# Gate products by groups of 32 tokens, turned by VectorE, in a windowed attention with a routed mixture of experts

## The chip, the cores and the metric

The kernel runs on one core of a Trainium2 chip. A core has five engines with their own instruction streams: TensorE (matmuls, PE in the profile, with its weight loads as PEld), VectorE (DVE), ScalarE (ACT), GpSimd (POOL) and SyncE (SP, which here only issues DMAs). SBUF is the working memory with 128 partitions, PSUM the memory into which TensorE writes. The metric is the time of one execution in microseconds (us); lower is better.

## What is computed

Sliding-window causal attention over 8 batches, 8 heads, 576 tokens and 64 dimensions a head, and on its output x (4608 tokens of 512 values) a mixture of eight experts with one expert for each token. Which one it is follows from two products of x with small weights: eight logits, and a local gate that says whether the token keeps the expert of the token before it.

```python
rel = pos[:, None] - pos[None, :]
mask = (rel >= 0) & (rel < window)            # window = 64
attn = softmax(where(mask, scale * q @ k.T, -1e9))
x = (attn @ v), heads side by side            # (B, S, 512)
logits = x @ w_gate                           # 8 of them
local_gate = sigmoid(x @ w_local)
for b, s:
    fresh_e = argmax(logits[b, s])
    e = fresh_e if s == 0 or local_gate[b, s] < 0.5 else prev_e
    prev_e = e
    out[b, s] = softmax(logits[b, s])[e] * (relu(x[b, s] @ w1[e]) @ w2[e])
```

## The kernel before

**Stages.** Attention comes first, over nine chunks of 512 tokens (`sc` from 0 to 8), each in four units of two heads (`hp` from 0 to 3). The router then makes places for the tokens, and the experts run over blocks of 256 gathered tokens, the first of them while the router still works on the rest. The order of the instructions on TensorE, ScalarE and SyncE is the order in which attention's code issues them; the instructions of VectorE and GpSimd are ordered by the scheduler of the framework.

**A unit.** `scores` makes k.T q for two heads in blocks of 64 by 64 (line 385), ScalarE takes the exponential (line 416) and VectorE multiplies by the mask (line 421; for seven units the mask is added by matmuls instead, line 400). `values` multiplies with v (line 431, 32 matmul records of a unit in pairs), and VectorE divides by the sums (lines 436, 439 and 441). Scores run two units ahead of values. `shift` copies v to a second tile that starts 64 tokens earlier, on ScalarE and GpSimd (lines 360 to 367).

**The gates, two ways.** Nine numbers are wanted for each token: eight logits and the local gate. For chunks 0 to 3, x itself is turned by TensorE (`turn`, line 302, copied by ScalarE at line 305), and `gates` multiplies it with the weights in four matmuls of 512 columns, one for each pair of heads (line 315). For chunks 4 to 8 (`GATED`), v is loaded already turned (`vtt`), and `gates` multiplies it with the weights of each head (line 317): 16 numbers a head, nine of them used, which then ride along with v through attention as nine more columns of `va` and `vb`. In both cases the four matmuls write to 32 PSUM partitions each, so that partitions hold gates and columns hold tokens. ScalarE copies this to `gs` (line 318).

**Turning them back.** The readers want tokens in partitions. `back` does four 128x128 transposes on TensorE (line 332). For chunks 0 to 3, `logits` sums the four pairs of heads on VectorE into `lt` (line 338); for chunks 4 to 8, `spread` has ScalarE copy the numbers into the free columns of `vb` and `va` (lines 346 to 348). The 64 tokens ahead of chunk 4 are treated alone by `gates_ahead` (lines 325 and 327) and `back_ahead` (lines 352 and 353), and a GpSimd copy puts them in place (line 345). All of these and the router's small products share one PSUM bank (`bank`).

**Places in the order.** For a chunk below 4, `gates` is issued at the end of the unit `hp` = 1 of the next chunk and `logits` in unit 2. For a gated chunk, `gates` is issued at the end of unit 2 of the chunk ahead of it and `spread` in unit 3, behind that unit's next scores. The router's first part (`first` and `gate`, lines 774 to 1025) is issued in small steps between units from chunk 4 on; its products at lines 812, 822 and 845 are TensorE instructions in the same stream, and its table at line 980 as well. It reads `lt`.

**Loads.** SyncE issues the loads of q, k, v and the turned v, up to three chunks ahead, and from about 112 us the first expert's weights (line 1182).

Of the kernel before, what the change touches and what calls it, by code (L numbers as in the profile page):

```python
# [8 lines left out]
F32 = mybir.dt.float32  # L9
# [4 lines left out]
Alu = mybir.AluOpType  # L14
AX = mybir.AxisListType
# [4 lines left out]
P = 128  # L20
B, H, S, DH = 8, 8, 576, 64
D = H * DH
E, F = 8, 1024
DK, FK = D // P, F // P
WIN = 64
# [35 lines left out]
SC = 4 * P  # L61
NSC = N // SC
HP = H // 2
KB = SC // WIN
SB = S // WIN
GW = 32
VX = DH + 1
VW = VX + E + 1
GATED = range(4, NSC)
# [8 lines left out]
def row_of(t):  # L78

    return t + (t >= ZR)  # L80
# [87 lines left out]
def attention(ctx, tc, ring, kq, v3, v4, vt, vh, xs, lt, ok, wg, wg2, ident, rt, ex):  # L168
# [14 lines left out]
    nc = tc.nc  # L183
    tp = ctx.enter_context(tc.tile_pool(name="at_t", bufs=1))
    cp = ctx.enter_context(tc.tile_pool(name="at_const", bufs=1))
    kp = ctx.enter_context(tc.tile_pool(name="at_k", bufs=3))
    pp = ctx.enter_context(tc.tile_pool(name="at_p", bufs=LEAD + 3))
    wk = ctx.enter_context(tc.tile_pool(name="at_work", bufs=2))
# [11 lines left out]
    def bank():  # L200

        return ps_e.tile([P, SC], F32, name="r")
# [3 lines left out]
    kqs, qts, kts, vts, vas, vbs = {}, {}, {}, {}, {}, {}  # L206
# [6 lines left out]


    vhs = tp.tile([P, HP, SC], F32, name="vtt")[:, :, :WIN]
    ahead = cp.tile([P, WIN], F32, name="ahead")
    ahead_t = cp.tile([P, H, E + 1], F32, name="ahead_t")

    def load(sc, parts):
        for part in parts:  # L220
# [16 lines left out]
    def until(i, x):  # L237

        nc.sync.dma_start(out=late[:, i:i + 1], in_=x)
# [57 lines left out]
    def turn(sc, x, half):  # L297

        r = pair()
        for i in range(2):  # L300
            for c in range(4):
                nc.tensor.transpose(r[:, i, c * P:(c + 1) * P],
                                    x[:, c, 2 * half + i].rearrange("p j d -> p (j d)"), ident)
        o = pp.tile([P, 2, SC], F32, name="p")
        nc.scalar.copy(o, r)
        vts.setdefault(sc, []).append(o)

    def gates(sc):

        r = bank()  # L310
        gs = wk.tile([P, SC], F32, name="gs", bufs=1)
        for hp in range(HP):
            h = slice(hp * GW, (hp + 1) * GW)
            if sc not in GATED:
                nc.tensor.matmul(r[h, :], lhsT=wg[:, hp, :], rhs=vts[sc][hp // 2][:, hp % 2], start=True, stop=True)
                continue
            nc.tensor.matmul(r[h, :], lhsT=wg2[:, hp, :], rhs=vts[sc][:, hp, :], start=True, stop=True)
        nc.scalar.copy(gs, r)
        return gs

    def gates_ahead():

        r = bank()
        for hp in range(HP):
            nc.tensor.matmul(r[hp * GW:(hp + 1) * GW, :WIN], lhsT=wg2[:, hp, :], rhs=vhs[:, hp, :],
                             start=True, stop=True)
        nc.scalar.copy(ahead, r[:, :WIN])

    def back(gs):
        r = bank()  # L330
        for c in range(4):
            nc.tensor.transpose(r[:, c * P:(c + 1) * P], gs[:, c * P:(c + 1) * P], ident)
        return r

    def logits(sc, gated):

        gt = back(gated).rearrange("p (c h g) -> p c g h", c=4, h=HP)[:, :, :E + 1]
        nc.vector.tensor_reduce(lt[:, 4 * sc:4 * sc + 4, :], gt, axis=AX.X, op=Alu.add)

    def spread(sc, gated):  # L340

        gt = back(gated).rearrange("p (c h g) -> p c h g", c=4, h=H)[:, :, :, :E + 1]
        g = slice(VX, VW)
        if sc == GATED[0]:
            nc.gpsimd.tensor_copy(vbs[sc][WIN:, 0, :, g], ahead_t[WIN:])
        nc.scalar.copy(vbs[sc][:WIN, :, :, g], gt[:WIN])
        nc.scalar.copy(vbs[sc][WIN:, 1:, :, g], gt[WIN:, :3])
        nc.scalar.copy(vas[sc][:, :, :, g], gt)

    def back_ahead():  # L350
        o = bank()[:WIN, :P]
        nc.tensor.transpose(o, ahead, ident)
        nc.scalar.copy(ahead_t[WIN:], o.rearrange("p (h g) -> p h g", h=H)[:, :, :E + 1])

    def shift(sc):

        va = vas[sc]
        vb = vbs[sc] = space("vb", sc)
        w = slice(width(sc - 1))
        nc.scalar.copy(vb[WIN:, 0, :, w], vas[sc - 1][WIN:, 3])  # L360
        nc.gpsimd.tensor_copy(vb[:WIN, :2], va[:WIN, :2])
        yield
        nc.scalar.copy(vb[WIN:, 1:3], va[WIN:, :2])
        yield
        nc.gpsimd.tensor_copy(vb[:WIN, 2:], va[:WIN, 2:])
        yield
        nc.scalar.copy(vb[WIN:, 3], va[WIN:, 2])

    def shift_first(half):

        va, h = vas[0], slice(4 * half, 4 * half + 4)
        if not half:
            vbs[0] = space("vb", 0)
            nc.gpsimd.memset(vbs[0][WIN:, 0], 0.0)
        nc.gpsimd.tensor_copy(vbs[0][:WIN, :, h], va[:WIN, :, h])
        nc.scalar.copy(vbs[0][WIN:, 1:, h], va[WIN:, :3, h])
# [78 lines left out]
    moves, gated, turned, old = (), None, None, None  # L455
# [3 lines left out]
    def step(free=True):  # L459
        nonlocal pause, side, trip  # L460
        pause -= HALF

        if side and pause <= 0.0 and (free or not trip):
            w, trip = next(side, (0.0, None))
            pause = max(pause, -HALF) + w
            if trip is None:
                side = ()
                if ex.jobs:
                    ex.rows(ex.jobs[0], -1)

    for i, (sc, hp) in enumerate(units):
        if hp == 0:
            x, g = wk.tile([P, 4, HP, 2, DH], F32, name="x"), None
            if sc in GATED:
                g = wk.tile([P, 4, HP, 2, E + 1], F32, name="g")

        if 1 < i < len(units) - LEAD:
            ps[units[i + LEAD]] = scores(*units[i + LEAD])
        if hp == (0 if sc else 3) and sc + 1 < NSC:
            moves = shift(sc + 1)  # L480
        for _ in range(2 if sc else 4):
            next(moves, None) if moves else None

        if hp == 3 and sc + 1 in GATED:
            spread(sc + 1, gated)
        elif (sc, hp) == (1, 3):
            gates_ahead()
        elif (sc, hp) == (2, 3):
            back_ahead()
        if hp == 3 and sc not in GATED:  # L490
            turn(sc, x, 0)
            old = x
        elif sc and sc - 1 not in GATED:
            if hp == 0:
                turn(sc - 1, old, 1)
            elif hp == 2:
                logits(sc - 1, turned)

        if side is None and 4 * sc >= C1 and hp >= 2:
            side = rt.first(bank)  # L500
        step(not (hp == 3 and sc + 1 in GATED))
        values(sc, hp, ps.pop((sc, hp)), x, g)
        if i < 2:
            ps[units[i + LEAD]] = scores(*units[i + LEAD])
        if i == 0:
            shift_first(1)
            until(1, allr[:1, 0, 0, 0, :1])
            load(2, [pairs[0], whole, pairs[1]])
            nc.sync.dma_start(out=vhs, in_=vh)
            load(3, pairs)  # L510
        if i == 2 * HP:
            with tc.issue_after(masked[-1].ins):
                rt.prepare()
                build_bias()
        if hp == 1 and sc and sc - 1 not in GATED:
            turned = gates(sc - 1)
        if hp == 2 and sc + 1 in GATED:
            gated = gates(sc + 1)
        if 0 < sc < NSC - 2 and hp == 0:
            load(sc + 2, [whole])  # L520
        if 0 < sc < NSC - 3 and hp == 1:
            load(sc + 3, pairs)
        if hp == 2 and sc + 2 in GATED:
            load(sc + 2, ["turned"])
        if (sc, hp) == (NSC - 3, 3):
            ex.jobs = [ex.weights({}, -1, ("w1",), lambda: until(2, allr[:1, sc, hp, 0, :1]))]
            if side == ():
                ex.rows(ex.jobs[0], -1)
        step(not (hp == 2 and sc + 1 in GATED))
        if (sc, hp) == (NSC - 2, 1):  # L530
            ex.weights(ex.jobs[0], -1, ("w2",), lambda: until(3, allr[:1, sc, hp, 0, :1]))
        if hp == HP - 1:
            if sc in GATED:
                nc.vector.tensor_reduce(lt[:, 4 * sc:4 * sc + 4, :], g.rearrange("p c h j e -> p c e (h j)"),
                                        axis=AX.X, op=Alu.add)
            nc.gpsimd.dma_start(out=xs[row_of(sc * SC):row_of(sc * SC) + SC, :D].rearrange("(c p) d -> p c d", p=P),
                                in_=x.rearrange("p c h j d -> p c (h j d)"))
# [1081 lines left out]
```

## Time and profile before

| | us |
|---|---|
| median of three runs | 644.74 |
| lowest and highest | 644.02, 646.02 |
| the profiled execution | 642.1 |
| its span, first to last instruction | 640.0 |
| TensorE busy | 615.6 |
| VectorE busy | 402.3 |
| ScalarE busy | 200.6 |
| attention's last values (line 431) end at | 133.5 |

The profile is of one execution. Times in it run from the start of the span. A row of the timeline gives the start, the duration, the engine, the line, the operation, the tiles it writes and reads, and in brackets how long the engine was idle before it and what ended that. "issue" in this place means that no semaphore, and so no other work of the program, ended the wait. A matmul's end is modelled, so for the time that TensorE spends on a group the start of the next group is the better guide. Engines overlap; what counts is the chain that cannot start earlier. A float32 matmul shows as two weight loads and two matmuls, a float32 transpose as one of each.

### The profile page before, as it was taken

The numbers are of one execution on the slowest core, as the hardware profiler recorded it, in microseconds if no ns is written. First come the engines' busy times: TensorE is split into PE (matmuls) and PEld (weight loads), VectorE is DVE, ScalarE is ACT, GpSimd is POOL, SyncE is SP. The second block draws the span as 40 slices with busy tenths as digits, with TensorE's granted clock in tenths as the row PEclk, the third lists the DMA queues.
The fourth block names the chain that finished last, engine by engine and source line by source line (L and its number), as shares of the span: only waits on it lengthen the run. The fifth ranks groups of instructions, "written<-read, shape, count | busy, mean of one in ns | idle before, by whom it ended". The sixth has DMA issues, their size and how long they took to land. (4 is left out here: it accounts for less than half of the span.)

```text
span 640.0 us, 14994 instructions
## 1 busy us (share of the span) xinstructions
PE 615.6 (96%) x6367; PEld 544.2 (85%) x6367; DVE 402.3 (63%) x752; ACT 200.6 (31%) x368; POOL 133.1 (21%) x132
## 2 busy tenths in 40 slices
PE   8889998899999999999999999999999999999995
PEld 7777777788889999978997999887997998899994
DVE  6676588879968775273654683362917752886730
ACT  3766765612572122113120312021211221213120
POOL 5422112430103202120302120211312022111101
PEclk9999998999999999999999999999999999999998
DMA  9999996969757645786958665769768556956501
GB/s 338 416 418 406 385 366 241 348 236 337 237 171 246 244 166 198 242 316 236 387 189 291 218 234 212 259 235 367 263 228 324 185 199 232 379 167 225 209 17 38
DMA packets 29318, 166.43 MB, mean 260 GB/s; under 512 B 8451, under 2 KB 9497, under 8 KB 20026
## 3 DMA queue, kind: packets, MB, share of 16 engines
q1 hardware_dynamic: 20394, 135.54, 58.4%
q0 software_dynamic: 8848, 29.85, 12.2%
q8 instruction: 52, 0.85, 0.5%
q14 instruction: 24, 0.20, 0.1%
HBM read 146.18 MB, written 19.59 MB: 259 GB/s over the span
## 5 line engine op out<-in xcount | busy, mean ns | idle before, releaser
L1394 POOL DMA_INDIRECT out_dram<-y,idx x36 | 41.1, 1141 | 339.1 <-DVE y L1327 196.5
L1318 PE MATMUL hp<-ws,hs 128*128 128x256 f32 x384 | 88.7, 380 | 0.0
L1318 PEld LDWEIGHTS hp<-ws,hs 128*128 128x128 f32 x384 | 72.6, 190 | 10.5 <-issue 0.8
L1268 PE MATMUL hp<-xs,ws 128*128 128x128 f32 x672 | 79.6, 275 | 0.0
L1268 PEld LDWEIGHTS hp<-xs,ws 128*128 128x128 f32 x672 | 77.3, 192 | 0.0
L1327 DVE SCALAR_TENSOR_TENSOR y<-hp,xg,kept 128x256 f32<-128x256 f32 x48 | 22.6, 482 | 74.2 <-issue 47.0
L1414 PE MATMUL hp<-xt,w 128*64 128x64 f32 (+2 forms) x640 | 66.2, 276 | 0.0
L1414 PEld LDWEIGHTS hp<-xt,w 128*128 128x128 f32 (+1 forms) x640 | 60.8, 170 | 4.1 <-issue 0.7
L1318 PE MATMUL hp<-w,h 128*128 128x256 f32 x256 | 61.1, 382 | 0.0
L1162 POOL DMA_INDIRECT xg<-xs,gx x40 | 50.3, 1258 | 45.6 <-issue 37.4
L1279 DVE TENSOR_TENSOR h<-hp,keep 128x512 f32<-128x512 f32 x42 | 28.6, 690 | 48.1 <-PE hp L1268 48.0
L1268 PEld LDWEIGHTS hp<-xt,w 128*128 128x128 f32 x448 | 53.2, 192 | 2.7 <-issue 1.3
L1268 PE MATMUL hp<-xt,w 128*128 128x128 f32 x448 | 54.7, 275 | 0.0
L1318 PEld LDWEIGHTS hp<-w,h 128*128 128x128 f32 x256 | 47.2, 190 | 6.3 <-issue 0.4
L431 PE MATMUL xo<-vb,p 128*64 128x74 f32 (+1 forms) x576 | 44.5, 230 | 7.0 <-issue 2.9
L416 ACT ACTIVATE p<-sp 128x512 f32<-128x512 f32 x72 | 39.2, 595 | 38.0 <-PE sp L385 35.9
L385 PEld LDWEIGHTS sp<-w 64*64 64x64 f32 x1296 | 38.7, 138 | 12.1 <-issue 8.5
L421 DVE TENSOR_TENSOR p<-p,mask 128x1024 f32<-128x1024 f32 x29 | 36.1, 1245 | 19.5 <-ACT p L416 19.3
L431 PEld LDWEIGHTS xo<-vb,p 128*64 128x64 f32 x576 | 38.9, 138 | 9.9 <-issue 4.4
L385 PE MATMUL sp<-w 64*64 64x128 f32 (+1 forms) x1296 | 43.8, 270 | 2.6 <-issue 1.5
L431 PE MATMUL xo<-va,p 128*64 128x74 f32 (+1 forms) x576 | 44.5, 230 | 1.2 <-issue 1.2
L1280 ACT ACTIVATE h<-h 128x512 f32<-128x512 f32 x42 | 26.3, 630 | 59.1 <-DVE h L1279 59.1
(280 smaller groups left out, 955.0 us busy)
## 6 DMA issues: line engine op xcount, KB each, us to landing
w<-in_w_dram SPq DMA_DIRECT2D x42, 2048.0 KB, 9.2
w<-in_kq_dram SPq DMA_DIRECT2D x17, 1024.0 KB, 8.7
w<-in_w_dram SPq DMA_DIRECT2D x24, 512.0 KB, 9.3
xs<-x POOLq DMA_DIRECT2D x9, 1024.0 KB, 9.5
va<-in_v_dram SPq DMA_DIRECT2D x5, 1184.0 KB, 8.9
vtt<-in_vt_dram SPq DMA_DIRECT2D x5, 1024.0 KB, 7.2
va<-in_v_dram SPq DMA_DIRECT2D x3, 1040.0 KB, 12.2
va<-in_v_dram SPq DMA_DIRECT2D x2, 520.0 KB, 6.8
```

The costliest lines, as they stand in the source:

```text
L385: nc.tensor.matmul(sp[j][c * WIN:(c + 1) * WIN, a:b], lhsT=kt[h, hp, block * WIN:(block + 1) * WIN], rhs=qt[h, hp, a:b], start=not biased, ...
L416: nc.scalar.activation(p[:, j], sp[j], Act.Exp, scale=DH ** -0.5)
L421: masked.append(nc.vector.tensor_tensor(p, p, m.to_broadcast([P, 2, SC]), op=Alu.mult))
L431: nc.tensor.matmul(xo[par * WIN:(par + 1) * WIN, j, s * VW:s * VW + n], lhsT=p[:, j, b * WIN:(b + 1) * WIN], rhs=w[:, s, 2 * hp + j, :n], ...
L1162: asked = self.nc.gpsimd.indirect_dma_start(out=x, out_offset=None, in_=self.xs[:rows, :], in_offset=bass.IndirectOffsetOnAxis(ap=gx[:, s: ...
L1268: nc.tensor.matmul(out[:, m, :], lhsT=a[:, kk, m * P:(m + 1) * P], rhs=b[:, kk, :], start=start and m + kk == 0, stop=stop and (m, kk) == ...
L1279: nc.vector.tensor_tensor(o, x, y, op=add)
L1280: nc.scalar.activation(o, x if y is None else o, Act.Relu)
L1318: nc.tensor.matmul(out, lhsT=a[:, m, :], rhs=b[:, m, :], start=start and m == 0, stop=stop and m == FK // 2 - 1, skip_group_check=True)
L1327: nc.vector.scalar_tensor_tensor(y[i][:, j * w:(j + 1) * w], x, pw[i], y2, Alu.mult, Alu.add)
L1394: self.nc.gpsimd.indirect_dma_start(out=self.out[:, :], out_offset=bass.IndirectOffsetOnAxis(ap=st["idx"][:, s:s + 1], axis=0), in_=y, in_ ...
L1414: nc.tensor.matmul(hp[a, i, :], lhsT=st["w1"][:, kk, m * P:(m + 1) * P][:, a], rhs=st["xt"][:, kk, :n], start=(kk == 0), stop=(kk == DK - 1))
```

## The change

The gate products are made so that VectorE's transpose of blocks of 32 by 32 suffices to turn them. The 512 tokens of a chunk are taken as 4 x 4 x 32 (c, q, t): a matmul takes the tokens of one q, 128 of them, and writes the 32 gates of a pair of heads to the PSUM partitions of that q. That makes sixteen matmuls of 128 columns in place of four of 512. For chunks 0 to 3 the four pairs of heads add up in PSUM, in 128 columns. One VectorE transpose reads PSUM and writes `gs` with tokens in partitions. `back`, `back_ahead` and ScalarE's copies of the gates go. `logits` becomes one ScalarE copy from `gs`, `spread` copies from `gs` in place of PSUM, and `gates_ahead` makes eight matmuls of 32 columns and a VectorE transpose of 64 partitions.

```diff
-    ahead = cp.tile([P, WIN], F32, name="ahead")
-    ahead_t = cp.tile([P, H, E + 1], F32, name="ahead_t")
+    ahead = cp.tile([P, P], F32, name="ahead")
...
     def gates(sc):
-        r = bank()
-        gs = wk.tile([P, SC], F32, name="gs", bufs=1)
+        r, gs = bank(), wk.tile([P, SC], F32, name="gs", bufs=1)
         for hp in range(HP):
-            h = slice(hp * GW, (hp + 1) * GW)
-            if sc not in GATED:
-                nc.tensor.matmul(r[h, :], lhsT=wg[:, hp, :], rhs=vts[sc][hp // 2][:, hp % 2], start=True, stop=True)
-                continue
-            nc.tensor.matmul(r[h, :], lhsT=wg2[:, hp, :], rhs=vts[sc][:, hp, :], start=True, stop=True)
-        nc.scalar.copy(gs, r)
+            x = vts[sc][:, hp] if sc in GATED else vts[sc][hp // 2][:, hp % 2]
+            x = x.rearrange("p (c q t) -> p q c t", c=4, q=4)
+            for q in range(4):
+                a = slice(q * GW, (q + 1) * GW)
+                if sc in GATED:
+                    nc.tensor.matmul(r[a, hp * P:(hp + 1) * P], lhsT=wg2[:, hp, :], rhs=x[:, q], start=True, stop=True)
+                else:
+                    nc.tensor.matmul(r[a, :P], lhsT=wg[:, hp, :], rhs=x[:, q], start=hp == 0, stop=hp == HP - 1,
+                                     skip_group_check=True)
+        if sc in GATED:
+            nc.vector.transpose(gs.rearrange("p (c h g) -> p h c g", c=4, h=HP),
+                                r.rearrange("p (h c t) -> p h c t", c=4, h=HP))
+        else:
+            nc.vector.transpose(gs[:, :P], r[:, :P])
         return gs

     def gates_ahead():
         r = bank()
         for hp in range(HP):
-            nc.tensor.matmul(r[hp * GW:(hp + 1) * GW, :WIN], lhsT=wg2[:, hp, :], rhs=vhs[:, hp, :],
-                             start=True, stop=True)
-        nc.scalar.copy(ahead, r[:, :WIN])
-    def back(gs):
-        r = bank()
-        for c in range(4):
-            nc.tensor.transpose(r[:, c * P:(c + 1) * P], gs[:, c * P:(c + 1) * P], ident)
-        return r
+            for i in range(2):
+                a = slice(WIN + i * GW, WIN + (i + 1) * GW)
+                nc.tensor.matmul(r[a, hp * GW:(hp + 1) * GW], lhsT=wg2[:, hp, :], rhs=vhs[:, hp, i * GW:(i + 1) * GW],
+                                 start=True, stop=True)
+        nc.vector.transpose(ahead[WIN:], r[WIN:, :P])

     def logits(sc, gated):
-        gt = back(gated).rearrange("p (c h g) -> p c g h", c=4, h=HP)[:, :, :E + 1]
-        nc.vector.tensor_reduce(lt[:, 4 * sc:4 * sc + 4, :], gt, axis=AX.X, op=Alu.add)
+        nc.scalar.copy(lt[:, 4 * sc:4 * sc + 4, :], gated[:, :P].rearrange("p (c g) -> p c g", c=4)[:, :, :E + 1])

     def spread(sc, gated):
-        gt = back(gated).rearrange("p (c h g) -> p c h g", c=4, h=H)[:, :, :, :E + 1]
+        gt = gated.rearrange("p (c h g) -> p c h g", c=4, h=H)[:, :, :, :E + 1]
         g = slice(VX, VW)
         if sc == GATED[0]:
-            nc.gpsimd.tensor_copy(vbs[sc][WIN:, 0, :, g], ahead_t[WIN:])
+            nc.gpsimd.tensor_copy(vbs[sc][WIN:, 0, :, g],
+                                  ahead[WIN:].rearrange("p (h g) -> p h g", h=H)[:, :, :E + 1])
...
-    def back_ahead():
-        o = bank()[:WIN, :P]
-        nc.tensor.transpose(o, ahead, ident)
-        nc.scalar.copy(ahead_t[WIN:], o.rearrange("p (h g) -> p h g", h=H)[:, :, :E + 1])
...
-        elif (sc, hp) == (2, 3):
-            back_ahead()
```

## The prediction

> **What bounds the kernel now.** I read the page first, then TensorE's idle times, then stretches cut where TensorE stood still. The page says that TensorE is busy nearly all the time and that a queue of its own brings instructions: 52 packets of 0.85 MB in all, 16 KB each.
>
> ```profile
> PE 615.6 (96%) x6367; PEld 544.2 (85%) x6367; DVE 402.3 (63%) x752; ACT 200.6 (31%) x368; POOL 133.1 (21%) x132
> ...
> q8 instruction: 52, 0.85, 0.5%
> ```
>
> The change lies wholly in attention, the first 131 us. The waits of TensorE (matmuls; engine, line, who ended it: us, times, longest) are few, and the largest one is of kind "issue": TensorE waited for nothing that the profile shows.
>
> ```profile
> PE xo L431 <- issue: 4.1, 4, 1.8
> ...
> PE xo L431 <- DVE x L441: 2.5, 1, 2.5
> ...
> PE sp L385 <- issue: 1.5, 2, 1.1
> ...
> PE r L822 <- DVE loc L817: 0.9, 1, 0.9
> PE r L812 <- ACT va L348: 0.6, 1, 0.6
> PE hp L1268 <- DVE h L1279: 0.5, 2, 0.2
> ```
>
> Where do the "issue" waits stand? In the timeline they cut groups in the middle: nothing that a data dependence would choose.
>
> ```profile
> 33.91 0.27 PE L431 MATMUL xo<-vb,p 128*64 128x65 f32 x1 [0.65 <-issue]
> ...
> 39.90 0.27 PE L385 MATMUL sp<-w 64*64 64x64 f32 x2 [1.09 <-issue]
> ...
> 122.94 0.22 PE L431 MATMUL xo<-va,p 128*64 128x74 f32 x1 [1.19 <-issue]
> ```
>
> I asked for the stretches from one such restart to the next (us; then PE and PEld with their instructions; the last two columns are the DMA share and GB/s).
>
> ```profile
> 27.71:33.91 6.20, 5.55 (x128) 4.20 (x128) 3.23 (x5) 3.78 (x7) 1.70 (x2) 1.00 1.01 423
> 33.91:39.90 5.99, 4.90 (x127) 4.30 (x128) 3.31 (x6) 2.80 (x5) 1.91 (x2) 1.00 1.02 423
> 39.90:52.24 12.34, 11.66 (x255) 9.48 (x255) 10.64 (x34) 8.73 (x14) 1.74 (x4) 1.00 1.01 415
> 122.94:129.11 6.17, 4.42 (x127) 4.03 (x127) 4.71 (x9) 2.17 (x4) 0.81 (x1) 1.00 1.02 409
> ...
> 52.24:121.60 69.36, 63.91 (x1528) 51.80 (x1528) 51.59 (x146) 45.22 (x80) 19.39 (x18) 0.98 0.93 339
> ```
>
> Each stretch holds 254 to 256 of TensorE's instructions, matmuls and weight loads together (the third holds two such blocks), and a packet of that queue, 0.85 MB / 52, would be 256 instructions of 64 bytes. Between 31.2 and 32.5 us, just ahead of the restart at 33.91, one passes:
>
> ```profile
> q8 instruction: 1, 0.02, 5.1%
> ```
>
> So I read the stalls as TensorE waiting for its next 256 instructions while the DMA engines are full. From 27.71 to 52.24 us a block costs 24.53/4 = 6.13 us however quickly TensorE works it off, 24 ns an instruction. From 52.24 to 121.60 us 3056 instructions, with some semaphore waits twelve blocks, take 69.36/12 = 5.78 us each, with no such stall: here TensorE's work, VectorE's chain and the fetch run at nearly one pace. After 115 us the experts' weights are loaded and the fetch binds again.
>
> **What the change does to TensorE.** One gate stage and what follows it, in the timeline of all engines and then in that of TensorE:
>
> ```profile
> 62.62 0.16 PEld L317 LDWEIGHTS r<-vtt,wg2s 128*32 128x32 f32 x8
> 62.62 1.07 PE L317 MATMUL r<-vtt,wg2s 128*32 128x512 f32 x8
> ...
> 63.62 0.99 PEld L385 LDWEIGHTS sp<-w 64*64 64x64 f32 x36 [0.84 <-issue]
> 63.62 1.13 PE L385 MATMUL sp<-w 64*64 64x128 f32 x36
> ...
> 64.67 0.42 PEld L332 LDWEIGHTS r<-ident,gs 128*128 128x128 f32 x4
> 64.67 0.66 PE L332 MATMUL r<-ident,gs 128*128 128x128 f32 x4
> ...
> 65.92 1.23 DVE L421 TENSOR_TENSOR p<-p,mask 128x1024 f32<-128x1024 f32 x1 [1.64 <-ACT p L416]
> ...
> 31.76 0.66 PE L332 MATMUL r<-ident,gs 128*128 128x128 f32 x4
> ...
> 32.14 0.27 PE L332 MATMUL r<-ident,gs 128*128 128x128 f32 x1
> 32.34 0.27 PE L431 MATMUL xo<-vb,p 128*64 128x65 f32 x1
> ```
>
> Removed: four transposes, in whose place nothing could start for 32.34 - 31.76 = 0.58 us. In nine stages that is 5.2 us of TensorE's time.
>
> Replaced: four matmuls of 512 columns by sixteen of 128. The old ones took 63.62 - 62.62 = 1.00 us. The new ones stream as many columns over the same four column groups, but are 64 instructions where the old were 16 (each float32 matmul shows two loads and two matmuls). The scores behind them issue 72 instructions in 64.67 - 63.62 = 1.05 us, 14.6 ns each; 64 of them make 0.93 us. The other end is eight rounds of the 0.27 us of a lone 128-column matmul, 2.2 us, if rounds do not overlap; the scores, which overlap, are the nearer row. I take 1.00 us, no change.
>
> So a stage goes from 16 + 8 to 64 instructions, 40 more; nine stages make 360. The first chunk's earlier gates go from 16 + 2 to 32, 14 more. Together 374, or 1.46 blocks.
>
> **The other engines.** No row shows VectorE's transpose. Near it are copies and products of the same sizes:
>
> ```profile
> L1197 DVE COPY xt<-tp 128x512 f32<-128x512 f32 x5 | 3.2, 682 | 0.0
> ...
> L439 DVE TENSOR_TENSOR g<-xo,allr 128x72 f32<-128x72 f32 x20 | 4.6, 232 | 0.5
> ...
> L318 ACT COPY gs<-r 128x512 f32<-128x512 f32 x9 | 5.3, 585 | 7.4 <-PE r L317 5.8 <-PE r L315 1.6
> ...
> L338 DVE TENSOR_REDUCE lt<-r 128x36 f32<-128x144 f32 x4 | 1.2, 306 | 2.9 <-PE r L332 2.9
> ...
> L327 ACT COPY ahead<-r 128x64 f32<-128x64 f32 x1 | 0.2, 220 | 0.0
> ```
>
> I take 0.68 us for 128x512, five times (bounds 0.59, ScalarE's copy of the same tile, and 1.23, the mask product of twice the size; the copy from PSUM by the same engine is the nearest row), and 0.3 us for 128x128, four times, against the 0.31 us of the reduction that goes. ScalarE loses nine copies of 0.585 us and gains four of about 0.22 us; it is 31% busy, so I count nothing. The new waits: VectorE's transpose waits for the gates, and behind it the next mask stands; in the stage above VectorE idles 1.64 us ahead of that mask, which covers 0.68. ScalarE's copies of the gates now wait for VectorE where they waited for TensorE; behind them stand copies and exponentials of a later unit. The PSUM bank is free sooner, so L812's 0.6 us goes, but the router's numbers that L812 and L822 carry come from VectorE, which is late instead.
>
> Two places hand savings to VectorE:
>
> ```profile
> 81.53 0.21 DVE L436 RECIPROCAL allr<-xo 128x8 f32<-128x8 f32 x1 [1.09 <-PE xo L431]
> ...
> 84.38 0.17 PE L822 MATMUL r<-ident,loc 14*1 14x14 f32 x1 [0.93 <-DVE loc L817]
> ...
> 102.18 0.28 PE L431 MATMUL xo<-vb,p 128*64 128x74 f32 x1 [2.52 <-DVE x L441]
> ...
> 100.00:105.00 5.00, 2.82 (x54) 2.67 (x58) 4.97 (x17) 1.87 (x4) 0.75 (x1) 0.76 0.55 219
> ```
>
> At 84.38 VectorE had idled 1.09 us shortly before; 0.68 of transpose plus TensorE coming 0.58 us sooner use that up, so the stage ahead of it saves nothing. At 102.18 TensorE already waits 2.52 us for VectorE: that stage's 0.58 us is lost, and its transpose lengthens the wait by 0.68. Given back: 0.58 + 0.58 + 0.68 = 1.84 us. The granted clock is 0.76 there after the wait; I count nothing for a longer one.
>
> **The sum by stretches.** To 52.24 us, two stages and the early gates: 94 instructions at 24 ns, +2.25 us; TensorE's saving is not felt, since the fetch sets the pace. From 52 to 115 us, six stages: -6 x 0.58 + 1.84 = -1.64 us; but 240 more instructions in 1.64 us less leave 67.7/12.9 = 5.25 us for a block. A block's fetch costs at most 5.78 us there on average, so the loss is between 0 and 12.9 x 0.53 = 6.8 us; I take a sixth, 1.1 us, because no stall shows there today. The DMA load is lower too:
>
> ```profile
> DMA packets 2729, 14.57 MB, mean 416 GB/s; under 512 B 742, under 2 KB 742, under 8 KB 1254
> ...
> DMA packets 2501, 15.97 MB, mean 380 GB/s; under 512 B 234, under 2 KB 234, under 8 KB 1002
> ```
>
> (20 to 55 us and 55 to 97 us.) That makes -0.5 us. After 115 us, one stage: 40 x 24 ns = +0.95 us. Sum: 2.25 - 0.5 + 0.95 = **+2.7 us**. Behind attention the list of waits has nothing over the 0.5 us of L1268, so a delay passes through to the end. The profiled execution took 642.1 us (span 640.0), 2.6 below the median of 644.74; I carry the difference to the median: **647.4 us**.
>
> **Rivals.** *The fetch stays hidden.* Then TensorE's work decides: -9 x 0.58 + 1.84 = -3.4 us, 641.3. It wins if a block costs under 5.25 us; for it speaks that twelve blocks run without a stall, against it the stalls at 6.0 to 6.2 us. [...]
>
> *The fetch gives way.* A slower pace asks less of the DMA engines, and an early block falls from 6.13 to 5.78 us: 4.37 x 5.78 - 24.53 = +0.7, the middle -0.5, the end between -0.58 and +0.95, say +0.2: +0.4 us, 645.1. Against it: the early transfers are asked for well ahead and keep the queues full.
>
> *The fetch binds throughout.* All 12.9 blocks at 5.78 us: 2.25 + 6.8 - 1.64 + 0.95 = +8.4 us, 653.1.
>
> That the sixteen matmuls do not run four abreast is the 2.2 us end above: nine times 1.2 us, +10.8 us. I leave it inside the tail.
>
> **How the numbers follow.** Forecast 0.38 (its own range 645.3 to 649.5), hidden 0.24, gives way 0.26, binds throughout 0.12. A measurement of this kernel tells 0.3%, 1.9 us, from no change. Of the forecast I put 0.06 within that; of the second rival 0.02 below it. Faster 0.26, same 0.30, slower 0.44. The range 641.3 to 651.5 leaves out half of the first rival and two thirds of the third.
>
> **What would show it.** Right: in the profile after, restarts "<-issue" inside groups, more of them than now and now also between 52 and 115 us, 256 instructions apart, in sum well over the 5.6 us of the two rows above; q8 with one or two packets more; the sixteen matmuls in about 1.0 us. VectorE's transpose near 0.68 us and the wait at L431 near 102 us longer. Wrong: no "issue" waits between 52 and 115 us and an attention that ends before 129 us; gates of over 1.2 us; or a transpose above 1 us, which would make VectorE the bound.

## The result and the profile after

The changed kernel takes **651.86 us** (median of six runs, 649.62 to 654.65) against 644.79 us (median of six, 643.69 to 646.76) for the kernel before: a ratio of 1.0109, with a 95% interval of 1.0079 to 1.0139, or 7 us slower. The forecast was 647.4 us with a range to 651.5: the sign was right, the loss was two and a half times as large. The profiled execution of after is the slowest of its six (654.65 us, span 652.7), 2.8 us above their median, and that of before (642.1 us, span 640.0) lies 2.7 us below its own. So the two traces differ by 12.6 us where the medians differ by 7.1, and a difference read between them is too large by some us.

What was added is there to the instruction. The page of after, busy times and TensorE's instruction queue (packets, MB):

```profile
PE 616.0 (94%) x6554; PEld 550.0 (84%) x6554; DVE 405.5 (62%) x758; ACT 196.9 (30%) x361; POOL 131.5 (20%) x132
...
q8 instruction: 54, 0.88, 0.5%
```

187 matmuls and 187 loads more, 374 together, and two packets more. One gated stage in the timeline of after shows the sixteen matmuls from 66.12 to 67.13 us, 1.01 us like the four, and no transposes on TensorE behind the scores:

```profile
66.12 0.81 PEld L316 LDWEIGHTS r<-vtt,wg2s 128*32 128x32 f32 x32
66.12 1.08 PE L316 MATMUL r<-vtt,wg2s 128*32 128x128 f32 x32
...
67.13 1.12 PE L382 MATMUL sp<-w 64*64 64x128 f32 x36
...
67.56 0.67 DVE L321 STREAM_TRANSPOSE gs<-r 128x512 f32<-128x512 f32 x1
```

VectorE's transposes by shape, 20 to 145 us (count, busy us, mean ns):

```profile
L321 DVE STREAM_TRANSPOSE gs<-r 128x512 f32<-128x512 f32 x5 | 3.5, 703 | 3.6 <-PE r L316 3.6
...
L324 DVE STREAM_TRANSPOSE gs<-r 128x128 f32<-128x128 f32 x4 | 1.2, 302 | 0.0
```

So every operation costs what the forecast gave it, 0.70 and 0.30 us on VectorE among them. The loss stands between the operations. TensorE's waits in after up to 150 us (line, who ended it: us, times, longest):

```profile
PE xo L428 <- issue: 6.5, 6, 1.5
PE sp L382 <- issue: 3.7, 3, 1.8
PE xo L428 <- DVE x L438: 3.7, 3, 2.3
...
PE r L316 <- issue: 2.3, 1, 2.3
...
PE r L975 <- issue: 1.8, 1, 1.8
PE r L817 <- DVE loc L812: 1.4, 1, 1.4
...
PE tp L1191 <- issue: 0.7, 1, 0.7
...
PE xo L301 <- issue: 0.2, 1, 0.2
```

Waits that nothing of the program ended, "issue", were 5.9 us before and are 15.2 us now. Four of the restarts, in the timeline:

```profile
70.59 0.13 PEld L428 LDWEIGHTS xo<-va,p 128*64 128x64 f32 x1 [1.20 <-issue]
...
80.95 0.13 PEld L428 LDWEIGHTS xo<-vb,p 128*64 128x64 f32 x1 [0.62 <-issue]
...
86.52 0.19 PEld L428 LDWEIGHTS xo<-va,p 128*64 128x64 f32 x2 [1.27 <-issue]
...
130.59 0.36 PEld L316 LDWEIGHTS r<-vtt,wg2s 128*32 128x32 f32 x11 [2.56 <-issue]
```

The first three lie where before had no such stall. Each of the four follows a packet of the instruction queue, and so does every other: in the fourteen traces of this case TensorE has 130 stalls of this kind of 0.3 us or more between 14 and 150 us, and each ends 1.2 to 1.6 us after such a packet has ended (in before and after 19 of them, at 1.26 to 1.58 us). Stretches between restarts (PE and PEld with their counts, granted clock, DMA share) hold one block of 256 instructions, or two:

```profile
46.27:52.46 6.19, 4.39 (x127) 3.85 (x128) 5.17 (x12) 3.02 (x6) 0.00 (x0) 1.00 1.03 418
70.59:80.95 10.36, 9.35 (x256) 8.25 (x256) 4.52 (x11) 7.33 (x12) 2.99 (x3) 1.00 0.91 336
80.95:86.52 5.57, 4.39 (x129) 3.84 (x129) 4.35 (x16) 2.88 (x8) 0.00 (x0) 1.00 1.01 377
```

In the last row 4.39 us of TensorE's work lies in 5.57 us: the block waits for its fetch. The whole of attention from 20 us to its last values, in before and then in after:

```profile
20.00:134.04 114.04, 101.69 (x2400) 83.52 (x2395) 83.11 (x217) 72.28 (x123) 29.07 (x28) 0.99 0.95 362
```

```profile
20.00:144.60 124.60, 101.31 (x2580) 89.09 (x2580) 85.91 (x223) 68.18 (x116) 29.54 (x28) 0.96 0.88 332
```

Attention ends 10.56 us later in this execution. TensorE is busy for the same time (-0.38) and idle for 10.94 us more; 9.3 of these are the waits "issue". That the busy time has not fallen, though nine times 0.58 us of transposes went, is in part the clock (the last column but two): it is 0.96 where it was 0.99, since attention in after has three stretches of 3.41 us at half clock and in before one. More of that below.

Behind attention the delay passes through: at the experts' activations from 137 to 527 us of before, after is 10.56 to 10.60 us behind. One place then adds 1.6 us: three stalls in a row in the experts' last part (553.23 us in after, line 1409). They stand in six of the ten traces of kernels with the right gates, but not in `twice_vector`, which has after's instructions on TensorE. Their cause is open, and so is whether the change has a part in them.

### The profile page after: what moved, and what is told of

Read it like the earlier page. It is cut to its first block, busy times and chain, and to the rows that moved or that the text cites. A ratio compares the mean times of both kernels' runs of the same rounds, so it can differ in the third digit from the quotient of the medians.

```text
span 652.7 us, 15365 instructions
## 1 busy us (share of the span) xinstructions
PE 616.0 (94%) x6554; PEld 550.0 (84%) x6554; DVE 405.5 (62%) x758; ACT 196.9 (30%) x361; POOL 131.5 (20%) x132
## 5 line engine op out<-in xcount | busy, mean ns | idle before, releaser
L1157 POOL DMA_INDIRECT xg<-xs,gx x40 | 48.1, 1202 | 45.8 <-issue 36.5
L428 PE MATMUL xo<-vb,p 128*64 128x74 f32 (+1 forms) x576 | 47.2, 236 | 8.9 <-DVE x L438 3.7
L428 PEld LDWEIGHTS xo<-vb,p 128*64 128x64 f32 x576 | 40.9, 143 | 13.5 <-issue 5.5
L428 PE MATMUL xo<-va,p 128*64 128x74 f32 (+1 forms) x576 | 46.8, 236 | 3.5 <-issue 3.4
## 6 DMA issues: line engine op xcount, KB each, us to landing
xs<-x POOLq DMA_DIRECT2D x9, 1024.0 KB, 11.6
```

What stands on the lines that cost most here:

```text
L428: nc.tensor.matmul(xo[par * WIN:(par + 1) * WIN, j, s * VW:s * VW + n], lhsT=p[:, j, b * WIN:(b + 1) * WIN], rhs=w[:, s, 2 * hp + j, :n], ...
L1157: asked = self.nc.gpsimd.indirect_dma_start(out=x, out_offset=None, in_=self.xs[:rows, :], in_offset=bass.IndirectOffsetOnAxis(ap=gx[:, s: ...
```

## The experiments

The theory: TensorE waits for its next 256 instructions, so instructions count and not work. The rivals: VectorE's transpose in a chain with little room; the sixteen matmuls or TensorE's work as such. Times are medians; "end" is the start of attention's last reciprocal in the profile (before: 133.52 us, after: 144.08), and "issue" the sum of those waits of TensorE between 20 and 145 us.

| kernel | us | before beside it | ratio (95%) | end | issue |
|---|---|---|---|---|---|
| before (median of six) | 644.79 | | | 133.52 | 5.9 |
| after | 651.86 | 644.79 | 1.0109 (1.0079 to 1.0139) | 144.08 | 15.2 |
| four_wide | (1011.6) | | | 131.89 | 7.5 |
| sixteen_scalar | (1021.2) | | | 145.42 | 13.8 |
| pad_many | 648.61 | 643.12 | 1.0110 (1.0070 to 1.0150) | 139.78 | 7.5 |
| pad_few | 645.98 | 643.12 | 1.0051 (1.0033 to 1.0068) | 137.60 | 6.0 |
| early_only | 647.64 | 645.11 | 1.0053 (1.0028 to 1.0078) | 136.77 | 11.6 |
| middle_only | 648.08 | 645.11 | 1.0044 (1.0025 to 1.0064) | 137.46 | 11.7 |
| light_before | (1013.8) | | | 131.98 | 5.0 |
| light_after | (1017.7) | | | 138.01 | 12.3 |
| tight_only | 648.70 | 644.03 | 1.0061 (1.0039 to 1.0083) | 137.81 | 10.2 |
| roomy_only | 646.96 | 644.03 | 1.0050 (1.0026 to 1.0074) | 136.01 | 9.7 |
| after_refilled | 651.54 | 644.03 | 1.0129 (1.0087 to 1.0171) | 138.86 | 9.2 |
| twice_vector | 649.07 | 642.64 | 1.0090 (1.0071 to 1.0108) | 142.51 | 15.2 |

Times in brackets are of kernels with altered gates: their tokens spread over the experts in another way, and a further pass follows that makes the total over 1,000 us. Only attention is compared there.

**Fewer instructions: `four_wide`.** In `gates` of after:

```diff
-            x = x.rearrange("p (c q t) -> p q c t", c=4, q=4)
-            for q in range(4):
...
+            a = slice(hp * GW, (hp + 1) * GW)
+            nc.tensor.matmul(r[a], lhsT=(wg2 if sc in GATED else wg)[:, hp, :], rhs=x, start=True, stop=True)
```

> The changed kernel with the four old matmuls of 512 columns in place of the sixteen of 128: 16 instructions of TensorE a stage instead of 64, 432 fewer in nine stages (gates_ahead keeps its 32); VectorE's transpose, ScalarE's copies and the missing four transposes stay as changed. Left out: the gates land with other tokens, and in the first four chunks the sum over head pairs. Theory of the fetch (the cost of the change is its additional instructions): 72 fewer than before remain, the stalls at every 256th instruction between 52 and 115 us go, and the time falls below before's 644.8, to 639 to 643. Theory of VectorE (its transpose, in a chain that is nearly the bound, costs the time): the instructions do not matter, TensorE streams as many columns, and it stays at 650 to 653.

Attention ends at 131.89 us, 12.2 us earlier than after and 1.6 earlier than before, with VectorE's transposes in place. Its waits:

```profile
PE xo L422 <- issue: 3.9, 3, 2.5
PE sp L376 <- issue: 3.4, 5, 1.3
PE xo L422 <- DVE x L432: 2.6, 2, 2.0
```

The issue waits halve, the waits for VectorE stay. 48 instructions a stage are the difference (against before it has 58 fewer in all, the early gates counted). Part of the 12.2 us is the clock: attention here has no stretch at half clock where after has three. TensorE's issue waits are 7.7 us less and its busy time 4.9 us less. Against the expectation not all stalls between 52 and 115 us go: two of 0.4 and 0.7 us stand at 94 and 99 us.

**No transpose on VectorE: `sixteen_scalar`.** `nc.vector.transpose` in `gates` becomes `nc.scalar.copy`.

> The changed kernel with the sixteen matmuls, but a plain copy by ScalarE from PSUM where VectorE transposed (nine places; the early gates keep their transpose). Left out: the transpose, so the gates land with other tokens. TensorE's instructions are those of the change. Theory of the fetch: 650 to 653, as with VectorE's transpose, and stalls 256 instructions apart between 52 and 115 us. Theory of VectorE: without 5 x 0.66 + 4 x 0.3 = 4.5 us of VectorE's time it falls to about 641 to 645.

The end is at 145.42 us, no earlier than after's, and the issue waits are 13.8 us. Taking VectorE's transposes away gains nothing that this trace shows. But it is a single profile, and attention has six steps of 3.41 us at half clock in it where after has three, which could hide a gain of up to 5 us. So a second run asked from the other side.

**Twice the transpose: `twice_vector`.** The transpose in `gates` of after is written twice.

> The changed kernel with VectorE's transpose done twice in each of the nine stages, the second over the first: 5 x 0.66 + 4 x 0.3 = 4.5 us more for VectorE, TensorE's instructions unchanged. Theory that the changed kernel waits for its instructions: VectorE has room beside the stalls and it costs 0 to +1.5 us over the changed kernel, most of it at the one or two waits for VectorE near 107 and 112 us. Theory that VectorE's chain sets the pace: +3 to +4.5 us.

Measured: +6.4 us over before by the medians (+5.8 by the ratio), where after had +7.1. The second transposes are 4.7 us more on VectorE, and they cost nothing that these runs show: 3 us over after lies outside the two intervals.

**Instructions or work: `pad_many` and `pad_few`.** In `gates` of before, ahead of its matmuls, the one or the other:

```diff
+        for n in range(10):
+            nc.tensor.matmul(r[:GW, :8], lhsT=wg[:, 0, :], rhs=ident[:, :8], start=True, stop=True)
```

```diff
+        for c in range(4):
+            nc.tensor.transpose(r[:, c * P:(c + 1) * P], ident, ident)
```

> The kernel before, with ten matmuls of 8 columns ahead of each stage's gates into the same bank: 40 instructions more in each of nine stages, 360 in all, about the number that the change adds; the four transposes, ScalarE's copy and all else stay. At the scores' 14.6 ns an instruction they are 0.58 us of TensorE a stage, 5.3 us in nine. Theory of the fetch: where it binds an instruction costs 24 ns, so 8.6 us or more over before, 653 to 656, with stalls at every 256th instruction between 52 and 115 us. Theory of VectorE: only TensorE's own 5.3 us or less, part of it beside VectorE's chain, 646 to 650.

> The kernel before, with four more transposes of 128 columns ahead of each stage's gates into the same bank: 0.58 us of TensorE a stage like the ten small matmuls, but 8 instructions in place of 40, 72 in all. Theory of the fetch: 2 x 8 x 24 ns at the early stages, where the fetch sets the pace, and up to 0.58 us in each of the six between, +3 to +4.5 us, 648 to 649, clearly less than the ten small matmuls, and no stalls at 256 instructions between 52 and 115 us. If instructions do not matter, the two additions cost the same.

In the traces the ten matmuls take 0.62 us of a stage and the four transposes 0.59. Nearly the same work costs 2.9 us as 72 instructions and 5.5 us as 360 (by the ratios 3.3 and 7.1). So instructions cost something of their own. Where they do can be read from attention's reciprocals, each beside the same one in before. At the last of chunk 2 (52.85 us in before) `pad_many` is 1.4 us further behind than `pad_few`, and the 64 more instructions that it has there make 1.5 us at 24 ns. From there to the first of chunk 7 (114.81 us) both lose the same 1.8 us, though `pad_many` has 240 more instructions there and `pad_few` 48. (Before has a stretch at half clock in that part and the two have none, so their work costs more than the 1.8.) So `pad_many` missed what the theory of the fetch expected (653 to 656): its issue waits are 7.5 us, and it shows no stall between 52.3 and 115 us. There 24 ns an instruction is no price to multiply with. These instructions brought their own work: with 240 more of them and 6 x 0.58 us in the middle a block still has (69.36 + 3.5)/12.9 = 5.6 us of work, where the change leaves it 5.25. I read this as a block taking the longer of its work and its fetch; only the change brings the work clearly below the fetch.

**Where the loss arises: `early_only` and `middle_only`.** The old form, with `back` in `logits` and `spread`, stays where `sc` is not in `ROWS`, which is `range(2)` (with the new early gates) or `range(2, 8)`:

```diff
+        if sc not in ROWS:
+            for hp in range(HP):
+                h = slice(hp * GW, (hp + 1) * GW)
...
+            nc.scalar.copy(gs, r)
+            return gs
```

> The change in the two earliest stages (chunks 0 and 1) and in the early gates of chunk 4 alone; the other seven stages as before. 94 instructions of TensorE more. The recorded sum has +2.25 us for this part. If the fetch sets the pace here whatever TensorE works: +2 to +3 us over before, with stalls at the same places as before but longer. If a stall also halves the granted clock in the 3.4 us after it: +3 to +4.5. If VectorE's transposes are the cost: their 3 x 0.3 us, under +1.

> The change in the six stages of 52 to 115 us alone (chunks 2 to 7), the early gates in the old form; chunks 0, 1 and 8 as before. 240 instructions of TensorE more. The recorded sum has -0.5 us for this part, with 1.1 us lost to the fetch. If that loss was too small, the stalls between 52 and 115 us show here as well and it is +2 to +5 us over before (-1.64 with all of the 6.8 us lost is +5.2). If the loss in the changed kernel came only from the delay that the early stages hand on, it is -2 to 0 here.

Early: +2.5 us by the medians (+3.4 by the ratio). In its trace attention is 2.2 us behind before from 60 to 89 us, with no stretch at half clock. Middle: +3.0 (+2.8, interval 1.6 to 4.1). The middle was to gain 0.5. Its waits between 20 and 145 us:

```profile
PE xo L452 <- issue: 6.2, 6, 2.0
PE sp L406 <- issue: 3.3, 4, 1.4
PE r L327 <- issue: 1.8, 1, 1.8
...
PE xo L452 <- DVE x L462: 0.6, 1, 0.6
```

No delay of earlier stages is needed for these stalls. The trace has the 3.0 us as well, between the last reciprocal of chunk 2 and the first of chunk 7. TensorE's issue waits there are 5.7 us where before has none. Its waits for VectorE and ScalarE are 1.9 us less and its busy time is 0.9 us less, which leaves 2.9. Both traces have one stretch at half clock there, so these 3 us are not the clock's. Early and middle together make 5.5 of the 7.1 us. The rest, 1.6 us, is left for chunk 8 if parts add up, which the next two runs put in doubt; it was not run alone.

**Is there room? `tight_only` and `roomy_only`.** The same condition with `range(2, 6)` and `(6, 7)`. The reason came from the packets of before. A block's room is the time from the end of its packet to its first instruction, less the time from packet to restart that a stalled block shows. One packet that matters lies between 72.75 and 73.70 us, for the block that begins at 75.25 (72.7 to 73.75 us):

```profile
q8 instruction: 1, 0.02, 5.7%
```

In after the packet ahead of the restart at 80.95 ends at 79.53, and the one ahead of 86.52 at 85.20: 1.42 and 1.32 us. Against the 1.54 us of before at 75.25 that leaves 0.1 to 0.2 us of room.

> The change in chunks 2 to 5 alone, whose stages lie between 52 and 85 us. In the trace of before the packets for the blocks that begin at 63.81, 75.25 and 81.16 us land only 1.5 to 1.65 us ahead of the block, and a stalled block restarts 1.3 to 1.5 us after its packet: nearly no room. 160 instructions more. Reading by the room: most of the middle's loss is here, +2.5 to +4.5 us over before. If every one of the six stages loses alike, two thirds of middle_only's 3 us: +2.

> The change in chunks 6 and 7 alone, whose stages lie at 92 and 108 us. In the trace of before the packets for the blocks that begin at 93.25, 97.96, 106.27 and 111.55 us land 2.0 to 4.2 us ahead of the block: 0.5 to 2.7 us of room. 80 instructions more. Reading by the room: the four removed transposes count and the instructions do not, -1.2 to +0.3 us against before, and no new stall between 90 and 115 us. If every stage loses alike, a third of middle_only's 3 us: +1.

`tight_only` came as the reading by the room said: +4.7 us (+3.9 by the ratio). Its trace has stalls at the three blocks that were named ahead (63.81, 75.25 and 81.16 us in before), and one stretch at half clock more than before:

```profile
63.08 0.22 PE L452 MATMUL xo<-va,p 128*64 128x65 f32 x1 [1.36 <-issue]
...
75.20 0.22 PE L452 MATMUL xo<-va,p 128*64 128x74 f32 x1 [1.01 <-issue]
...
81.98 0.31 PE L327 MATMUL r<-vtt,wg2s 128*32 128x128 f32 x4 [2.39 <-issue]
```

`roomy_only` did not: +2.9 us (+3.2), where it was to be at zero or below. Its timeline shows where the gain went:

```profile
100.09 0.28 PE L452 MATMUL xo<-vb,p 128*64 128x74 f32 x1 [0.42 <-DVE x L462]
...
101.28 1.08 PE L406 MATMUL sp<-w 64*64 64x128 f32 x27
104.54 0.44 PE L406 MATMUL sp<-w 64*64 64x128 f32 x5 [2.18 <-issue]
```

The wait for VectorE that stood at 102.18 us in before, 2.52 us long, is 0.42 us here and ends 2.1 us earlier. But the next block's packet passes from 102.10 to 103.05 us as in before (102.06 to 103.01), and at 104.54 TensorE gives the time back, waiting 2.18 us for it. The room that I had read there was made by the wait itself. This explains the missing gain and not all of the loss: at the first reciprocal of chunk 7 `roomy_only` is 0.65 us behind before, and the other 1.8 us of the 2.5 at the end arise after 115 us, where its stages are those of before. That its 80 instructions shift the later blocks there is likely and not shown. The two runs add up to 7.6 us, and `middle_only` with the same six stages to 3.0, so stages are not priced one by one.

**Work into the stalls: `after_refilled`.** The four transposes of `pad_few`, now in `gates` of after.

> The changed kernel with four transposes of 128 columns ahead of each stage's gates into the same bank: the 0.58 us of TensorE's work a stage that the change took away comes back, with 8 instructions; nothing reads them. In before the same four cost 2.9 us in nine stages. Theory that the changed kernel waits for its instructions: the work fills stalls that are there anyway, and it costs +0.5 to +2 us over the changed kernel, clearly under 2.9, about 652.5 to 654 where before is 644.8. Theory that TensorE's work or VectorE's chain sets the pace: the same 2.9 us or more, up to 5.2.

+7.5 us over before by the medians, after had +7.1: 5.2 us of TensorE's work come back for 0.4 us. By the ratios it is 1.3 us, and the intervals are too wide to exclude the 2.9 of `pad_few`, so the cheapness is not certain. The waits tell where it went:

```profile
PE sp L384 <- issue: 5.4, 5, 1.5
PE xo L430 <- issue: 3.4, 4, 1.2
```

With 0.4 us at a third line, 9.2 us of issue waits in place of 15.2. A part of it is the clock: the mean granted clock of a run is 0.995 here and 0.990 in after, and attention has one stretch at half clock in the trace where after has three.

**Is it the load on the DMA engines? `light_before` and `light_after`.** Four loads of 1 MB are left out of each kernel:

```diff
-                vts[sc] = tp.tile([P, HP, SC], F32, name="vtt")
-                nc.sync.dma_start(out=vts[sc], in_=vt[GATED.index(sc)])
+                if sc == GATED[0]:
+                    vts[sc] = tp.tile([P, HP, SC], F32, name="vtt")
+                    nc.sync.dma_start(out=vts[sc], in_=vt[GATED.index(sc)])
+                    continue
+                vts[sc] = vts[GATED[0]]
```

> The kernel before without the four loads of 1 MB of the turned values for chunks 5 to 8: their gates are taken from chunk 4's tile, so the loads and the right gates of these chunks are left out. It is there to be compared with the same cut in the changed kernel, at the end of attention. All theories: no stall of TensorE between 52 and 115 us, attention's end 0 to 2 us earlier than before.

> The changed kernel with the same four loads left out, and the same gates wrong. Theory of the fetch (TensorE's next 256 instructions come late because the DMA engines are full): with 4 MB less between 55 and 115 us the stalls there become fewer and shorter, and from chunk 4 to chunk 7 the lag behind the kernel with the same cut grows by less than 1 us or shrinks, where with the loads it grew by 4. Theory that sixteen matmuls are slower work in themselves, or that VectorE's chain is late: the lag grows by the same 4 us.

Compared at the reciprocals, the lag of the one behind the other grows from 4.0 us at the start of chunk 4 to 5.5 at unit 2 of chunk 7; with the loads it grew from 4.4 to 8.7. That is less, but more than the 1 us expected, and the issue waits remain 12.3 us (5.0 in `light_before`). In that part the trace of after also has one stretch of low clock more than `light_after`, up to 1.7 us of the difference. So it is not settled how far the DMA load sets the fetch in the middle; 4 MB less did not make it short. The packet itself takes about as long with the queues nearly empty as with them full: 0.95 us in before from 102.06 us, at 67 GB/s, and 1.06 us from 31.36 us, at 433 GB/s. What sets the time ahead of it is open.

## Why the prediction was right or wrong

- **374 instructions, 1.00 us, 0.68 and 0.3 us.** Right: 374, 1.01 us, 0.70 and 0.30 us.
- **To 52.24 us, +2.25.** Right: `early_only` has +2.5 us, and its trace 2.2 us just behind that place. In the trace of after the lag there is 4.1 us, in part since a stretch at half clock begins at 53.99 us.
- **From 52 to 115 us, -0.5.** This is the step that failed: `middle_only` has +3.0. Its term "I take a sixth, 1.1 us, because no stall shows there today" was mis-sized. With the sum's -1.64 the loss must be 4.5 to 4.6 us, two thirds of the 6.8 that I had as its upper end. Read directly, the issue waits in that part of `middle_only` are 5.7 us, against none in before. I compared a mean of twelve blocks with a mean fetch. Block by block the trace of before had the answer: three of them began 0.1 to 0.3 us after the earliest moment that their packet allowed. "No stall shows" did not mean that there was room.
- **"I count nothing for a longer one"** (the low clock). Wrong. The mean granted clock of the runs fell from 0.995 (the runs of before beside `roomy_only`) to 0.990. At the 0.50 granted in the low stretches that is 0.005 x 650 / 0.5 = 6.5 us a run more at the low clock, at most 3.3 us of time; the two stretches that attention has more in the trace of after agree, with at most 3.4. How much of the 7 us this is cannot be told from the stalls ahead of it: `after_refilled` has the clock of before and the time of after.
- **VectorE's give-back, 1.84 us.** The waits for VectorE did grow, from 3.4 to 5.1 us, by 1.7. But in `middle_only` they fell to 2.2, so the 1.7 is a match by chance, and `twice_vector` shows that VectorE's transposes do not set the time. That the next fetch takes back what a shorter wait for VectorE gives is shown at one place only, 104.54 us of `roomy_only`.
- **After 115 us, +0.95.** Not run alone. By subtraction 1.6 us are left for it; in the traces the lag from the first reciprocal of chunk 7 to the end grows by 3.0 us in after, but also by 1.9 in `early_only`, which leaves chunk 8 as it was. So this term stays open.
- **The rivals.** "The fetch stays hidden" fell with the stalls at 70.59, 80.95 and 86.52 us. "The fetch gives way" fell too: the four early blocks of after, 27.31 to 52.46 us, take 6.29 us each, more than the 6.13 of before. "Binds throughout" came near the time with 653.1, and nearly had the mechanism, though not every block binds: the two from 70.59 to 80.95 us took 10.36 us with 9.35 of work. It had no term for the clock either, so that its time came so near is in part luck. The crossing from one block to the next was not hidden in after: 15.2 us of such waits in 125 us, up to 2.3 us at one boundary.

## What to carry to other kernels

Where a profile shows stalls of kind "issue" a fixed number of instructions apart (one or two blocks of 254 to 258 here), a change that trades work for instructions on that engine can lose twice: it fetches more, and it has less work to do while it fetches. Here 374 instructions more and nine times 0.58 us of transposes less came with a loss of 7 us, in part the clock's. So count instructions beside microseconds. Judge the room block by block, from the end of a block's instruction packet to the block's start, and not from means; room that stands behind a wait goes when the wait goes. And a microsecond saved ahead of a late fetch can come back as a stall at the next block, as in `roomy_only` the 2.1 us saved at 102.18 us came back as 2.18 us at 104.54.

## What I had not expected of the hardware

**Half the clock after short stalls.** In attention the granted clock of after and before falls to 0.50 for 3.41 us at a time, and each time the 3.41 us ahead of it held little work of TensorE, 0.90 to 1.92 us. After, then before:

```profile
47.17:50.58 3.41, 3.41 (x112) 3.02 (x102) 2.67 (x6) 2.72 (x6) 0.00 (x0) 1.00 1.03 420
50.58:53.99 3.41, 1.60 (x27) 1.46 (x26) 1.59 (x3) 0.66 (x2) 0.00 (x0) 1.00 1.01 418
53.99:57.41 3.42, 3.42 (x61) 3.00 (x63) 2.12 (x3) 1.44 (x2) 0.96 (x1) 0.50 0.32 132
...
108.61:112.02 3.41, 1.15 (x40) 1.02 (x40) 3.41 (x11) 1.09 (x2) 0.00 (x0) 1.00 0.82 306
112.02:115.43 3.41, 3.41 (x60) 3.14 (x64) 2.62 (x9) 0.00 (x0) 0.00 (x0) 0.50 0.02 6
```

```profile
99.22:102.63 3.41, 0.90 (x34) 0.76 (x25) 3.38 (x11) 2.65 (x4) 0.20 (x1) 1.00 0.61 242
102.63:106.04 3.41, 3.41 (x64) 3.14 (x62) 3.08 (x13) 0.00 (x0) 0.55 (x1) 0.50 0.73 290
126.53:129.94 3.41, 1.66 (x52) 1.50 (x45) 2.85 (x5) 1.08 (x2) 0.00 (x0) 1.00 1.02 402
129.94:133.35 3.41, 3.41 (x80) 3.13 (x76) 2.04 (x6) 1.07 (x2) 0.00 (x0) 1.00 0.69 261
```

From 53.99 to 57.41 us 61 matmuls run where 112 ran in a full stretch. The starts in one trace lie on a grid of 3.41 us (53.99, 91.54 and 112.02 are 11 and 6 steps apart), so the same stall costs the clock or not by where it falls on the grid: the one of 1.8 us that ends at 52.46 us in after was followed by half clock, and one of 1.8 us that ends at 52.11 us in `early_only` was not. TensorE's instructions are the same in the two up to there. From the reciprocal at 46.60 us of before to that at 56.19, after then lost 1.4 us more than `early_only`, which I take as the price of the stretch.

The busy time ahead of a low stretch shows no sharp limit in these rows: 1.60 of 3.41 us was followed by half the clock, 1.66 of 3.41 us was not. I counted the steps of the grid at full clock in all fourteen traces, from 15 to 145 us. Nineteen were followed by half clock, all with at most 1.92 us busy. Every step with less than 1.60 us was, and between the two values it went either way. The step with 1.92 us, in after:

```profile
88.13:91.54 3.41, 1.92 (x50) 1.53 (x47) 3.38 (x7) 2.85 (x4) 1.82 (x3) 1.00 0.87 319
91.54:94.95 3.41, 3.41 (x66) 3.20 (x60) 1.49 (x7) 1.34 (x3) 0.00 (x0) 0.50 1.02 400
```

**More work, a better clock.** `pad_few` with its additional transposes has a mean granted clock of 0.998, where the runs of before beside it have 0.994, and its trace has no stretch at half clock in attention where before has one. That is a part of why its 5.3 us of work cost 2.9 us.
